# Contracting k and v over 128 rows instead of 64, with a new order of loads and new scheduler settings, in a fused linear attention and wave MLP kernel

## The chip, the cores and the metric

One Trainium2 chip, one of its cores. The metric is the device time of one execution in microseconds (us). A profile of one execution was taken for every kernel; its span (first to last instruction of the program) is some 1.8 us shorter than the device time. The tables give medians of all runs of a kernel. The experiments came with the kernel before in the same rounds, so kernels are compared by their ratios to it. PE is the matmul engine (PEld its weight loads), DVE the vector engine, ACT the scalar engine, POOL the GpSimd engine, SP the engine that issues the DMAs.

## The reference, cut to what matters

```python
# q, k, v: (8 batches, 8 heads, 576 tokens, 64), fp32
kv  = einsum('bhsd,bhse->bhde', k, v)      # 64x64 per head, contracts the 576 tokens
out = einsum('bhsd,bhde->bhse', q, kv)
x   = out / rms(out) * g_norm              # then (8, 576, 512)
theta = x @ w_theta
y = w_tok_r @ (x*cos(theta)) + w_tok_i @ (x*sin(theta))    # mixes the 576 tokens
u = x + y
result = u + relu(u @ w_ch)
```

The change touches the first line: 64 products of 576 tokens, in fp32, for 8 batches of 8 heads.

## The kernel before

The kernel is one static program. A scheduler in Python (`Weave`) takes tasks with a due time, engines, an assumed cost and what they need and use. It plays them through on a clock of its own, and so fixes the order of every engine's queue before anything runs. Where the scheduler believes PE idle in the first 40 us, it puts in a warm-up matmul (a `warm` task of 0.22 us that no one needs). The granted clock of the first 43.29 us is 1.00 with them in the trace of this kernel.

```python
PERIOD = 24.61
DUE = {"load": (-15.33, 2.93), ..., "attention": (1.6, 3.82), "norm": (12.64, 4.8), ...}   # cut
SLOTS = {..., "k": 6, "v": 6, "q": 6, ..., "wst": 8, ...}
class Weave:
    SLACK  = {"PE": 0, "ACT": 0.052, "DVE": 0.064, ...}
    MARGIN = {"PE": 0.011, "ACT": 0.06, "DVE": 0.119, ...}
```

k and v of a head pair are loaded with 64 partitions a head, 9 consecutive tokens a partition. Each head's product then runs in one 64x64 quadrant of PE; the two heads use the two quadrants of the diagonal.

```python
t = sb(kind, [P, NS, D], FP32, ...)            # NS = 9; partitions 0-63 head 0, 64-127 head 1
nc.sync.dma_start(out=t[:]..., in_=src[b, pair].rearrange("h (p j) d -> (h p) (j d)", j=NS))
...
for j in range(NS):                            # kv: 18 matmuls a head pair
    for r in range(2):
        half = slice(r * PH, (r + 1) * PH)
        nc.tensor.matmul(kvp[r*D:(r+1)*D, hp, :], st["k", b, hp][half, j, :],
                         st["v", b, hp][half, j, :], start=(j == 0), stop=(j == NS - 1))
weave.add(("kv", b, hp), [pe(0.6)], ...)       # assumed cost 0.6 us
```

x is turned (transposed on PE) in five pieces a batch; the fifth has 64 valid tokens and was turned with all 128 rows. The weights come in this order: batch 0, `w_theta`, the two mixers `w_tok`, batch 1, `w_ch`, batch 2.

## Time and profile before

| kernel before | |
|---|---|
| time, median of 4 runs | 242.91 us (242.85 to 243.21) |
| span of the profiled run | 241.2 us |
| first y matmul, last y matmul starts | 43.29 us, 232.94 us |
| kv groups (a head pair's kv), 32 of them | 36 PE instructions, 1.20 us each |

The first part of the profile page (busy us, share of the span, instructions) and its part 4 (the chain of work that ended last):

```profile
PE 233.1 (97%) x2789; PEld 160.3 (66%) x2789; DVE 183.3 (76%) x369; ACT 158.8 (66%) x297; POOL 86.3 (36%) x104
...
PE 92%; ACT 3%; DVE 3%; issue 0%; DVEq 0%
PE y L855 29%; PE kv L499 15%; PE vps L899 12%; PE th L768 11%; PE warm L284 9%; PE raw L535 4%; PE ups L890 4%; PE xTps L737 4%; PE th L773 2%; PE wTps L407 1%; ACT tr L811 1%; ACT tr L803 1%; PE qTps L469 0%; DVE f L784 0%; DVE ot L910 0%
```

PE is busy nearly always and is 92% of the chain. kv is 15% of it. The busy time in two stretches (columns: stretch, its length, then the busy us of PE, PEld, DVE, ACT and POOL with their instructions, granted clock, DMA share, GB/s):

```profile
68.40:79.00 10.60, 8.25 (x110) 5.81 (x109) 8.16 (x17) 7.39 (x16) 3.43 (x4) 1.00 0.95 323
79.00:198.00 119.00, 119.00 (x1529) 84.67 (x1527) 101.67 (x199) 88.09 (x161) 48.41 (x47) 1.00 0.66 190
```

In the long second stretch PE has no gap, and DVE, third in the row, is busy for 85% of the time. In the short first one PE loses 2.4 us. In the timeline of PE (start, duration, line, what, how many) a kv group and a turn of x look like this:

```profile
104.84 1.26 PE L499 MATMUL kv<-v,k 64*64 64x64 f32 x36
106.04 0.30 PE L890 MATMUL ups<-ident,uT 128*64 128x128 f16 x4
...
119.10 0.39 PE L737 MATMUL xTps<-ident,x 128*128 128x128 f16 x4
119.32 1.39 PE L855 MATMUL y<-wT,z 128*128 128x320 f16 x9
```

What an item takes from PE is the distance from its start to the start of the next, as durations overlap: 106.04 - 104.84 = 1.20 us for kv, 0.22 us for the turn. An fp32 matmul shows as two instructions, hence 36 for 18.

### The profile page before, as it was taken

To read this page: it belongs to the slowest core of one execution; us is meant where nothing else is said; L and a number is where in the kernel's file an instruction comes from. 1 tells how busy PE (TensorE), PEld (TensorE's weight loads), DVE (VectorE), ACT (ScalarE), POOL (GpSimd) and SP (SyncE) were. 2 spreads that over 40 slices of the span, in tenths; PEclk is the share of its full clock that TensorE was granted. 3 is DMA by queue.
4 is the path that set the end of the run, shared out by engine and by line. 5 is a ranking of instruction groups with operands and counts; after the bars stand their busy time and mean duration, and the time that the engine had idled before them with its cause. 6 is when DMAs were issued, how large, how long until landed. Compare 5 with 4: busy or idle time off the path is not lost.

```text
span 241.2 us, 6820 instructions
## 1 busy us (share of the span) xinstructions
PE 233.1 (97%) x2789; PEld 160.3 (66%) x2789; DVE 183.3 (76%) x369; ACT 158.8 (66%) x297; POOL 86.3 (36%) x104
## 2 busy tenths in 40 slices
PE   7999999999987999999999999999999999999993
PEld 2665556977655766776668766776676775765861
DVE  1267585288977889779897988997789868997652
ACT  2377677335885678647895868785858668788021
POOL 4005630354334560263363334433252605540000
PEclk9999999999999999999999999999999999999999
DMA  6995999974379748844796469974981512102314
GB/s 185 279 348 194 287 330 380 315 284 117 79 228 356 239 98 279 241 150 89 202 338 201 87 184 300 292 146 134 312 267 27 133 55 105 50 1 90 109 46 153
DMA packets 45375, 46.49 MB, mean 193 GB/s; under 512 B 21664, under 2 KB 30880, under 8 KB 45344
## 3 DMA queue, kind: packets, MB, share of 16 engines
q1 hardware_dynamic: 45280, 46.05, 62.7%
q8 instruction: 22, 0.36, 0.7%
q14 instruction: 9, 0.07, 0.1%
q0 software_dynamic: 64, 0.00, 0.0%
HBM read 33.06 MB, written 9.44 MB: 176 GB/s over the span
## 4 chain that ended last, share of the span: by engine, by line
PE 92%; ACT 3%; DVE 3%; issue 0%; DVEq 0%
PE y L855 29%; PE kv L499 15%; PE vps L899 12%; PE th L768 11%; PE warm L284 9%; PE raw L535 4%; PE ups L890 4%; PE xTps L737 4%; PE th L773 2%; PE wTps L407 1%; ACT tr L811 1%; ACT tr L803 1%; PE qTps L469 0%; DVE f L784 0%; DVE ot L910 0%; ACT sq L542 0%
## 5 line engine op out<-in xcount | busy, mean ns | idle before, releaser
L855 PE MATMUL y<-wT,z 128*128 128x320 f16 (+1 forms) x576 | 78.9, 286 | 1.5 <-DVE z L821 1.5
L855 PEld LDWEIGHTS <-z 128*128 128x128 f16 x576 | 53.7, 98 | 16.8 <-DVE z L821 2.0
L557 POOL TENSOR_TENSOR rt<-ss,mhalf 128x8 f32<-128x8 f32 x35 | 60.6, 1733 | 2.9
L863 DVE SCALAR_TENSOR_TENSOR uT<-y,gcol,xT 128x256 f16<-128x256 f32 (+1 forms) x64 | 32.7, 513 | 16.5 <-PE y L855 16.3
L553 POOL TENSOR_SCALAR ss<-ss 128x8 f32<-128x8 f32 x35 | 11.3, 323 | 94.4 <-DVE ss L546 93.8
L499 PEld LDWEIGHTS kv<-v,k 64*64 64x64 f32 x1152 | 36.1, 135 | 8.3 <-issue 6.1
L499 PE MATMUL kv<-v,k 64*64 64x64 f32 x1152 | 40.5, 221 | 0.0
L899 PE MATMUL vps<-wch,uT 128*128 128x512 f16 (+1 forms) x192 | 37.7, 344 | 0.0
L780 ACT ACTIVATE pt<-th,magic_t 128x512 f32<-128x512 f32 (+1 forms) x40 | 25.8, 644 | 18.0 <-PE th L768 17.2
L746 ACT ACTIVATE xT<-xTps,gcol 128x512 f16<-128x512 f16 (+1 forms) x36 | 22.9, 636 | 16.0 <-PE xTps L737 16.0
L768 PE MATMUL th<-wth,xT 128*128 128x512 f16 x128 | 32.8, 380 | 0.0
L784 DVE SCALAR_TENSOR_TENSOR f<-pt,th 128x512 f32<-128x512 f32 (+1 forms) x40 | 25.2, 629 | 9.0 <-ACT pt L780 8.9
L906 ACT COPY u<-ups 128x512 f16<-128x512 f16 (+1 forms) x40 | 21.3, 539 | 14.8 <-PE ups L890 14.5
L821 DVE TENSOR_TENSOR z<-x,tr 128x1024 f16<-128x1024 f16 (+1 forms) x40 | 25.2, 632 | 4.6 <-ACT tr L803 2.4
L910 DVE SCALAR_TENSOR_TENSOR ot<-vps,u 128x512 f32<-128x512 f32 (+1 forms) x40 | 25.1, 631 | 4.7 <-PE vps L899 2.2
L546 DVE TENSOR_REDUCE ss<-sq 128x8 f32<-128x512 f32 x36 | 24.3, 679 | 2.3 <-ACT sq L542 2.0
L569 DVE TENSOR_TENSOR x<-raw,rt 128x512 f16<-128x512 f32 x36 | 24.6, 683 | 1.3 <-POOL rt L557 1.1
L284 PE MATMUL warm<-kvbd 128*128 128x512 f16 x80 | 23.5, 411 | 1.7 <-DVE pio_t L248 1.5
L542 ACT ACTIVATE sq<-raw 128x512 f32<-128x512 f32 x36 | 21.1, 593 | 3.8 <-PE raw L535 3.8
L803 ACT ACTIVATE tr<-fa,pio_t 128x512 f16<-128x512 f32 x32 | 22.9, 719 | 0.8 <-DVE fa L791 0.2
L803 ACT ACTIVATE tr<-f 128x512 f16<-128x512 f32 x32 | 20.2, 632 | 2.9 <-DVE f L784 2.8
L899 PEld LDWEIGHTS <-uT 128*128 128x128 f16 (+1 forms) x192 | 14.2, 102 | 8.6 <-issue 0.6
(73 smaller groups left out, 217.0 us busy)
## 6 DMA issues: line engine op xcount, KB each, us to landing
k<-in_k_dram SPq DMA_DIRECT2D x32, 288.0 KB, 5.8
v<-in_v_dram SPq DMA_DIRECT2D x32, 288.0 KB, 5.8
q<-in_q_dram SPq DMA_DIRECT2D x32, 256.0 KB, 5.7
out_dram<-ot SPq DMA_DIRECT2D x32, 256.0 KB, 3.2
wmix<-in_moe_w_tok_r_dram SPq DMA_DIRECT2D x4, 288.0 KB, 6.7
wmix<-in_moe_w_tok_i_dram SPq DMA_DIRECT2D x4, 288.0 KB, 4.0
ql<-in_q_dram SPq DMA_DIRECT2D x8, 128.0 KB, 5.6
wst<-in_moe_w_theta_dram SPq DMA_DIRECT2D x4, 256.0 KB, 7.7
```

The costliest lines, as they stand in the source:

```text
L284: nc.tensor.matmul(t[:], kv_bd[1][:, 0, :], kv_bd[1][:].rearrange("p h c -> p (h c)"), start=True, stop=True,)
L499: nc.tensor.matmul(kvp[r * D:(r + 1) * D, hp, :], st["k", b, hp][half, j, :], st["v", b, hp][half, j, :], start=(j == 0), stop=(j == NS - 1),)
L557: nc.gpsimd.tensor_tensor(out=r[:], in0=t[:], in1=mhalf[:], op=ALU.pow)
L768: nc.tensor.matmul(t[:], xT[:, kc, :], wth[:, kc, :], start=(kc == 0), stop=(kc == NK - 1),)
L780: nc.scalar.activation(out=t[:], in_=st[th][:], func=AFT.Identity, bias=magic_t[:])
L784: nc.vector.scalar_tensor_tensor(out=t[:], in0=st[pt][:], scalar=MAGIC, in1=st[th][:], op0=ALU.subtract, op1=ALU.subtract,)
L803: nc.scalar.activation(out=t[:, which, :], in_=src[:], func=AFT.Sin, scale=-RAD, bias=0.0 if bias is None else bias[:],)
L821: nc.vector.tensor_tensor(out=t[:], in0=xb.unsqueeze(1).broadcast_to((P, w, C)), in1=st[tr][:, 0:w, :], op=ALU.mult,)
L855: nc.tensor.matmul(t[:], z[:, kc * P:(kc + 1) * P], wT[m][:, cols], start=(m == 0), stop=(m == NM - 1),)
L863: nc.vector.scalar_tensor_tensor(out=st["uT", b][:, kc, cols], in0=st[y][:], scalar=gcol[:], in1=st["xT", b][:, kc, cols], op0=ALU.mult, o ...
L899: nc.tensor.matmul(t[half], uT(kc), wch[:, kc, r * n:(r + 1) * n], start=(kc == 0), stop=(kc == NK - 1),)
L910: nc.vector.scalar_tensor_tensor(out=t[:], in0=st[vp][:], scalar=0.0, in1=st[u][:], op0=ALU.max, op1=ALU.add,)
```

## The change

Intent: PE is the limit, and a kv matmul in a quadrant uses only 64 of the 128 rows that could contract (64\*64 in its trace, where the matmuls of y show as 128\*128). Batches 1 to 7 load k and v over all 128 partitions with 4 tokens each (512 tokens), and the last 64 tokens as separate tails over 64 partitions; the other 64 partitions of the tail tiles stay zero. A pair then needs 10 matmuls for 18. Batch 0 keeps quadrants, as it would otherwise wait for a tail. Half of batch 1 is loaded ahead of the mixers, the tail of x is turned with 64 rows, and due times, slacks and costs of the scheduler are new.

```diff
-PERIOD = 24.61
+PERIOD = 24.57
     ... (15 of the 17 entries of DUE are new, e.g.)
-    "mixers": (20.83, 4.62),
-    "phase": (19.07, 4.95),
+    "mixers": (14.15, 5.87),
+    "phase": (19.49, 4.62),
-    "wst": 8,
+    "wst": 6,
+MIX_AFTER = 5        # mixers are loaded after head pair 1 of batch 1
+WCH_AFTER = 7
-    SLACK = {"PE": 0, "ACT": 0.052, "DVE": 0.064, ...}
-    MARGIN = {"PE": 0.011, "ACT": 0.06, "DVE": 0.119, ...}
+    SLACK = {"PE": 0.053, "ACT": 0, "DVE": 0.124, ...}
+    MARGIN = {"PE": 0.051, "ACT": 0, "DVE": 0.444, ...}
     ...
-                if kind == "q":
+                if kind == "q" or b > 0:         # [P, 2, NF, D]: 128 rows of NF = 4 tokens
     ...  (tails kl, vl: 128 KB each per batch, double-buffered)
+            if b > 0:
+                for j in range(NT):              # NT = 5: four of 512 tokens' rows, one tail
+                    for r in range(2):
+                        nc.tensor.matmul(
+                            kvp[r * D:(r + 1) * D, hp, :],
+                            st["k", b, hp][:, r, j, :] if j < NF else st["kl", b][:, 2 * hp + r, :],
+                            st["v", b, hp][:, r, j, :] if j < NF else st["vl", b][:, 2 * hp + r, :],
+                            start=(j == 0), stop=(j == NT - 1))
+                return
-        weave.add(("kv", b, hp), [pe(0.6)], ...
+        weave.add(("kv", b, hp), [pe(0.8 if b else 1.2)], ...
     ...  (turn of x)
+            rows = P if ti < NF else T
-                    t[:, kc, :], st[f"x{b}_{ti}"][:, kc * P:(kc + 1) * P], ident16[:],
+                    t[:, kc, :], st[f"x{b}_{ti}"][0:rows, kc * P:(kc + 1) * P], ident16[0:rows, 0:rows],
```

## The prediction

The 33 ns a matmul that it takes for the shorter turn of x is an estimate, the rate of kv's 64-column matmuls (1.20 us over 36 instructions).

> **What bounds the kernel now.** TensorE. The page has PE busy 233.1 of 241.2 us (97%), DVE 76%, ACT 66%; the chain that ended last is 92% PE, at full clock: y 29%, kv 15%, vps 12%, th 11%, and 9% warm-up matmuls in the load-bound start. By windows, from 79 to 198 us PE is never idle, DVE is busy 101.7 of 119 us (85%), DMA share 0.66. Exceptions: the start (first y at 43.3 us), a hole from 68 to 79 us (PE loses 2.4 us, chain on ACT and DVE), the drain after 198 us (4 us lost).
>
> **What changes.** In the timeline each kv group (one head pair) is 36 PE instructions, two fp32 passes of 18 matmuls in 64x64 quadrants, and takes 1.20 us, 33 ns each. In batches 1 to 7 (28 of 32 groups) 128 rows contract: 10 matmuls, 20 instructions, in 128x64 column tiles.
> - At 33 ns a group takes 0.67 us. [...] This trace's 128x64 tiles do run together, with a surcharge: the x8 tail th takes 0.56 us, 140 ns a pair, against 107 ns at full th's rate (215 ns per 512 columns). I take 0.75 us, between 0.67 and the 0.8 of the diff's cost table (its 1.2 for quadrants agrees with the trace). Saving 0.45 us per group.
> - About 24 groups run after the first y, in the busy stretch: -10.8 us. Those of batch 1 among warm-ups save nothing.
> - Tail x turn, 64 moving columns for 128: 56 to perhaps 33 ns a matmul, x4 x7: -0.6 us.
> - Half of batch 1 ahead of the mixers: DMA had a gap there (20 to 25 us: share 0.49), which the loads fill; mixers land later, but PE gets batch 1's kv meanwhile. The order after has 81 warm-ups against 80. First y: 42 to 45.5 us; cost +1.
> - DMA: k, v go from 2304 B runs to 1024 B, plus 14 tails of 128 KB in 256 B runs (the q tail takes 5.6 us to land, as long as 256 KB of q). Steady share about 0.75; not binding.
> - DVE and ACT lose nothing. With the steady stretch 7% shorter DVE goes from 85% to about 92%: new PE gaps, +1.5 us. Better costs in the scheduler may close part of the 68 us hole: -0.5.
>
> Sum: -9.4 us, so 233.5 us, range 229.5 to 238.5. Chances: faster by over 2% (below 238.0) 0.88, within 2% 0.11, slower 0.01.
>
> **What would show it.**
> - kv groups of batches 1 to 7 as x20, 0.67 to 0.8 us each, batch 0 still 1.20; kv's share of the chain near 10%.
> - Steady period (kv group to the same group a batch later, 24.8 us now) 23.0 to 23.5 us.
> - DVE busy sum near 183 us, over 90% in the steady stretch; PE slightly below 97%, with small idle ending on DVE or ACT.
> - First y within 2 us of 43.3.
>
> **What would make it wrong.** [...] (2) DVE's in-order queue becoming the limit: period near 24 us. (3) Mixers so late that the first y slips 4 us. (4) 256 B tails delaying loads in the DMA-bound stretch from 25 to 50 us. (5) Fast side: 0.67 us groups and smaller holes, near 229 us.

## The result, and the profile after

| | before | changed |
|---|---|---|
| time, median of 4 runs | 242.91 us (242.85 to 243.21) | 232.13 us (230.75 to 233.36) |
| span of the profiled run | 241.2 | 230.3 |
| first y starts | 43.29 | 44.32 |
| last y starts | 232.94 | 221.88 |
| PE time of kv after the first y | 29.9 | 17.6 |
| PE idle after the first y | 2.5 | 3.0 |
| warm-ups | 80 | 81 |

The ratio is 0.9552 (95% interval 0.9498 to 0.9607). Ratios here are the mean time of one kernel's fast runs over that of the other's in the same rounds, so not quite the ratio of the quoted medians. The rows on PE are worked out from the starts in the trace: what an instruction takes is the distance to the next start, up to 0.30 us, and what exceeds that is called idle.

The first part and part 4 of the page of the changed kernel:

```profile
PE 220.8 (96%) x2342; PEld 145.8 (63%) x2342; DVE 185.2 (80%) x368; ACT 157.3 (68%) x298; POOL 88.0 (38%) x108
...
PE 73%; DMA 9%; DVE 6%; ACT 5%; POOL 3%; issue 1%; SPq 1%; DVEq 0%
```

Its stretches, in the same columns as before:

```profile
68.00:79.00 11.00, 8.29 (x106) 6.23 (x104) 8.49 (x19) 6.46 (x14) 4.60 (x6) 1.00 0.92 275
79.00:187.00 108.00, 107.57 (x1185) 72.40 (x1182) 98.88 (x195) 84.42 (x158) 46.41 (x45) 1.00 0.78 205
```

PE still has almost no gap in the long stretch, but DVE is now at 98.88 of 108 us, 92%. The chain is only 73% PE, for two reasons. In the first 25 us it now goes through the loads (21 us of DMA, the 9% above), where it went through warm-ups before, though PE itself lost next to nothing by waiting for k and v (under 1 us in the whole run). In the long stretch it is 78% PE, 11% DVE, 5% ACT and 4% POOL, where it was all PE before. The hole near 70 us is still there, 2.7 us large. The timeline of PE of the changed kernel, with its first y, two kv groups in a row, the tail turn of x, and a single kv group:

```profile
44.32 2.14 PE L893 MATMUL y<-wT,z 128*128 128x256 f16 x18
...
62.02 0.69 PE L524 MATMUL kv<-v,k 128*64 128x64 f32 x16
62.53 0.29 PE L524 MATMUL kv<-vl,kl 128*64 128x64 f32 x4
62.65 0.64 PE L524 MATMUL kv<-v,k 128*64 128x64 f32 x16
63.12 0.29 PE L524 MATMUL kv<-vl,kl 128*64 128x64 f32 x4
63.34 1.04 PE L806 MATMUL th<-wth,xT 128*128 128x512 f16 x4
...
87.93 0.29 PE L775 MATMUL xTps<-ident,x 64*128 64x64 f16 x4
88.15 1.04 PE L937 MATMUL vps<-wch,uT 128*128 128x512 f16 x4
...
93.84 0.69 PE L524 MATMUL kv<-v,k 128*64 128x64 f32 x16
94.36 0.29 PE L524 MATMUL kv<-vl,kl 128*64 128x64 f32 x4
94.58 1.04 PE L937 MATMUL vps<-wch,uT 128*128 128x512 f16 x4
```

A kv group is now 20 instructions. It takes 0.74 us when it stands alone (93.84 to 94.58), but two in a row take only 1.32 us (62.02 to 63.34), with the first at 0.63. The tail turn takes 0.22 us (87.93 to 88.15), exactly as long as a turn of 128 rows before, and where a th matmul runs ahead of it, that one takes 311 ns for 216.

Where the 11.0 us of span come from is a short sum. The first y comes 1.0 us later; kv after the first y takes 12.4 us less of PE (29.93 to 17.56); PE idles 0.5 us more; all other matmuls after the first y take 0.2 us less in sum, and what follows the last matmul 0.1 us more. One of the groups behind the 12.4 us moved ahead of the first y (25 groups ran after it before, 24 now).

The distances from start to start inside one group, worked out from the trace in ns (the last number is the distance to the next, full-width instruction), show what a group consists of:

```
64x64 quadrants, 36:   7, 100,  7, 52,  6, 52,  7, 51, ... 7, 52, 6 | 151
128x64 columns,  20:   7, 100,  6, 52,  7, 51,  7, 51, ... 7, 51, 7 | 154
```

Two instructions of a pair start 7 ns apart, and pairs follow every 58 ns in both forms. So a pair costs the same whether 64 or 128 rows contract. Added to that are about 0.15 us inside the group, at its first pair (107 for 58) and its last (161 for 58). Where a full-width turn runs ahead of it, that turn's last matmul takes 149 ns for 56 as well. Together it is about 0.24 us a group. Next to another half-width group these additions vanish: an exit takes 51 instead of 154 ns. So in these traces the additions come with a change of the tile shape. It is not the fp32 type: fp16 matmuls in 128x64 tiles between full-width ones pay the same at their ends (149 ns ahead of them, 152 after), and from the last of such fp16 matmuls to a kv group behind them it is 52 ns. 0.24 us is what one such change and the way back cost here.

### The profile page after: what moved, and what is told of

Read it like the earlier page. It is cut to its first block, busy times and chain, and to the rows that moved or that the text cites. A ratio compares the mean times of both kernels' runs of the same rounds, so it can differ in the third digit from the quotient of the medians.

```text
span 230.3 us, 5955 instructions
## 1 busy us (share of the span) xinstructions
PE 220.8 (96%) x2342; PEld 145.8 (63%) x2342; DVE 185.2 (80%) x368; ACT 157.3 (68%) x298; POOL 88.0 (38%) x108
## 3 DMA queue, kind: packets, MB, share of 16 engines
q1 hardware_dynamic: 59840, 46.05, 71.9%
## 4 chain that ended last, share of the span: by engine, by line
PE 73%; DMA 9%; DVE 6%; ACT 5%; POOL 3%; issue 1%; SPq 1%; DVEq 0%
PE y L893 27%; PE vps L937 11%; PE th L806 11%; PE kv L524 6%; DMA wst<-in_moe_w_theta_dram 4%; PE xTps L775 4%; PE ups L928 4%; PE warm L293 3%; DMA vl<-in_v_dram 3%; PE raw L572 3%; DMA v<-in_v_dram 2%; POOL rt L594 2%; ACT tr L849 2%; DVE x L606 2%; PE wTps L432 2%; PE th L811 1%
## 5 line engine op out<-in xcount | busy, mean ns | idle before, releaser
L590 POOL TENSOR_SCALAR ss<-ss 128x8 f32<-128x8 f32 x35 | 9.5, 271 | 85.2 <-DVE ss L583 84.6
L859 DVE TENSOR_TENSOR z<-x,tr 128x1024 f16<-128x1024 f16 (+1 forms) x40 | 27.0, 674 | 3.4 <-ACT tr L849 1.7
L524 PE MATMUL kv<-v,k 128*64 128x64 f32 x448 | 19.0, 227 | 0.0
L524 PEld LDWEIGHTS kv<-v,k 128*64 128x64 f32 x448 | 15.3, 137 | 5.6 <-issue 4.2
```

The costliest lines, as they stand in the source:

```text
L524: nc.tensor.matmul(kvp[r * D:(r + 1) * D, hp, :], st["k", b, hp][:, r, j, :] if j < NF else st["kl", b][:, 2 * hp + r, :], st["v", b, hp][ ...
L859: nc.vector.tensor_tensor(out=t[:], in0=xb.unsqueeze(1).broadcast_to((P, w, C)), in1=st[tr][:, 0:w, :], op=ALU.mult,)
```

## The experiments

There were twelve runs, one of them the changed kernel again. The kernel before, in the rounds of each call, had medians from 243.14 to 243.39 us. The theory to be tested: the row form is the gain, by shortening kv on a PE-bound chain. The rivals: the new scheduler settings, or the new order of loads.

### 1. The row form alone, all but the row form, and two small parts

The kernel before with only the row form and its tails (`a_kv_only`):

```diff
 # kernel before, plus: loads of k, v for b > 0 in 128 rows; tails; the 10-matmul loop
 weave.add(("kv", b, hp), [pe(0.6)], ...)      # cost, due times, slacks, order of loads as before
```

> The kernel before with the 128-row form of k, v in batches 1 to 7 and the two tails added, and nothing else: its order of loads, its due times, slacks and costs (0.6 us a kv group) stay. Theory (the row form is the gain; 24 groups of batches 1 to 7 after the first y, each 0.47 us shorter on PE, nearly all of it on the chain): 231 to 234 us, 9 to 12 us below the kernel before. Rival (the retuned schedule and the order of loads make half of the gain or more): 237 us or above.

The changed kernel with quadrants (`b_quadrants`):

```diff
-                if kind == "q" or b > 0:
+                if kind == "q":
-            if b > 0:
+            if False:
-[pe(0.8 if b else 1.2)]
+[pe(1.2)]                                      # and no tails
```

> The changed kernel with quadrants for k, v of all batches (288 KB loads, no tails, 36 PE instructions and a cost of 1.2 us a group), everything else as changed. Theory: the gain is gone, 241 to 245 us. Rival (retune and order of loads): it stays near the changed kernel, 233 to 238 us.

The changed kernel with the mixers ahead of batch 1 (`c_mix_first`), and with the tail of x turned by 128 rows (`d_full_turn`):

```diff
-MIX_AFTER = 5
+MIX_AFTER = 3
```

> The changed kernel with the mixers loaded before all of batch 1, as in the kernel before (one constant, 5 becomes 3). Theory (the order of loads only moves waits about in the start; the first y moved from 43.3 to 44.3 us with the change): within 1.5 us of the changed kernel, first y between 42 and 45 us. Rival (the loads ahead are needed because kv of batch 1 would come too late): 2 us or more slower, first y or the second batch's first y later by that.

```diff
-            rows = P if ti < NF else T
+            rows = P                            # and its cost 0.25 for 0.13
```

> The changed kernel with the tail x turned by 128 rows as in the kernel before (eight times 4 transposes at 56 ns a piece, 0.22 us). In the changed kernel's trace the 4 shorter ones take 39, 29, 29 and then 122 ns to the next matmul, 0.22 us as well, with perhaps 0.1 us lost in the matmul ahead of them. Theory now (a change of tile shape costs what the shorter stream saves): within 1 us of the changed kernel, rather faster than slower, tail x turn again 0.22 us. Rival (my prediction: 0.6 us saved by 64 rows): 0.6 us slower than the changed kernel.

| run | median us | ratio to before | first y | last y |
|---|---|---|---|---|
| row form alone | 238.55 | 0.9809 (0.9783 to 0.9834) | 42.49 | 229.14 |
| all but the row form | 242.16 | 0.9958 (0.9935 to 0.9981) | 44.05 | 231.74 |
| mixers first | 233.42 | 0.9607 (0.9568 to 0.9646) | 39.72 | 223.55 |
| tail x by 128 rows | 232.67 | 0.9570 (0.9545 to 0.9596) | 43.53 | 222.29 |

The row form alone missed what was expected of it: 4.6 us faster, not 9 to 12. Everything except the row form is worth 1.0 us. So neither the theory nor the rival holds alone; 4.6 + 1.0 is about half of the gain. In the row-form run PE spends 11.1 us less on kv after the first y (18.8 for 29.9) but idles 7.9 us there for 2.5. Its waits (who waited for whom: total us, times, longest) say on what:

```profile
PEld L889 <- DVE z L855: 6.7, 4, 2.3
...
PE y L889 <- DVE z L855: 5.6, 4, 2.0
```

The same wait of the kernel before, from its own list:

```profile
PE y L855 <- DVE z L821: 1.5, 1, 1.5
```

y of a batch needs the last z of that batch, and z comes late in DVE's queue, whose order is fixed. Of the 11.1 us, 5.4 came back as idle time of PE, most of it waits for z (5.6 us for 1.5). Another 2.7 came back as other matmuls that took longer; this profile has a dip of the clock to half from 74.2 us, 3.4 us long (see the last part of this section). What is left, and a first y 0.8 us earlier, is the 3.8 us by which the last y is earlier.

The order of loads, as far as the place of the mixers goes, is worth about 1.3 us by the ratios (0.9607 - 0.9554 times 243, with the changed kernel of experiment 2), and the two intervals overlap. With the mixers first, y even starts 4.6 us earlier, contrary to the 42 to 45 us expected, but the stretch from first to last y is 6.3 us longer. Turning the tail of x with fewer rows is worth nothing that can be seen: 0.957 and 0.955 overlap. Its 0.6 us in the prediction were not there, as the four shorter matmuls (39, 29, 29 ns apart) are followed by 122 ns to the next, 0.22 us in all, and the matmul ahead loses 0.09 us more.

### 2. Which setting, and fewer changes of the tile shape

> The changed kernel itself, unchanged, so that the others of this call have it on the same chip, and for its spread (230.75 to 233.36 us in four runs, where the kernel before stays within 0.4 us). Both theories: 231 to 233.5 us, ratio near 0.955.

```diff
 # changed kernel with PERIOD and DUE of the kernel before        (r_due)
```

> The changed kernel with the table of due times and the period of the kernel before; slacks, costs, order of loads and the row form stay as changed. The row form alone gave only 4.6 us of the 10.8, although its trace has kv 13.2 us shorter on PE: PE idled 5.6 us more, mostly before y, waiting for z on DVE. Theory A (the order of the work, set by the due times, lets the freed PE time reach the end): 235 to 239 us, most of 5 us lost. Theory B (the slacks and margins of the scheduler do it): within 1.5 us of the changed kernel.

```diff
 # changed kernel with SLACK and MARGIN of the kernel before      (r_slack)
```

> The changed kernel with the slacks and margins of the kernel before; all else as changed. Theory A (due times): within 1.5 us of the changed kernel. Theory B (slacks and margins): 235 to 239 us. If both this and the run with the old due times lose 2 us or more, the settings only work together and neither is the cause by itself.

```diff
+KVG = 2                                         # (kv_pairs)
+                for h in range(hp - KVG + 1, hp + 1):    # two head pairs in one task
                     for j in range(NT): ...
-[pe(0.8 if b else 1.2)]
+[pe(1.4 if b else 1.2)]
```

> The changed kernel with kv of two head pairs in one go (40 PE instructions, cost 1.4 us), due when the second pair was. In the changed kernel's trace a pair of instructions takes 58 ns in both forms, and entering and leaving the half-width form from full 128x128 costs about 0.24 us a group beyond that (the matmul ahead 149 instead of 56 ns, the first pair 107 instead of 58, the last to the next 154 instead of 52). If that is a cost of changing the tile shape, each double group takes 1.32 us from its first start, 14 changes fewer save 14 x 0.24 = 3.4 us of PE and, as two thirds to all of freed PE time reach the end only with matching due times, 0.5 to 3 us of the whole. Rival (the gaps belong to each group's first load, whatever ran before): double groups of 1.46 us or more, no gain.

| run | median us | ratio to before |
|---|---|---|
| changed kernel again | 232.66 (231.68 to 232.99) | 0.9554 (0.9530 to 0.9577) |
| old due times | 234.80 | 0.9649 (0.9620 to 0.9677) |
| old slacks and margins | 233.69 | 0.9606 (0.9587 to 0.9624) |
| kv of two head pairs in one go | 234.91 | 0.9648 (0.9622 to 0.9674) |

By the medians, old due times lose 2.1 us, old slacks 1.0. Neither reaches the 235 to 239 us that theory A or B asked for, though the old due times come close. With the old due times PE waits for x, 4.8 us before the turn of x for 0.7 in the changed kernel (this profile is of the slowest of the six runs). First the line of the run with old due times, then that of the changed kernel:

```profile
PE xTps L775 <- DVE x L606: 4.8, 5, 2.8
...
PE xTps L775 <- DVE x L606: 0.7, 2, 0.5
```

The double groups did what the changes of shape predict, and lost all the same. One of them in the timeline of that run, 82.61 to 83.93 = 1.32 us:

```profile
82.61 0.69 PE L526 MATMUL kv<-v,k 128*64 128x64 f32 x16
83.12 0.29 PE L526 MATMUL kv<-vl,kl 128*64 128x64 f32 x4
83.24 0.64 PE L526 MATMUL kv<-v,k 128*64 128x64 f32 x16
83.71 0.29 PE L526 MATMUL kv<-vl,kl 128*64 128x64 f32 x4
83.93 0.82 PE L811 MATMUL th<-wth,xT 128*128 128x512 f16 x3
```

Over the whole run, PE's time on kv fell from 25.6 to 23.1 us, and PE's idle rose from 5.3 to 8.9. That makes 1.1 us of the 2.2 lost; the order also has 4 more warm-ups (85), and this profile has the clock at half for 6.8 us from 71.4 us. The waits of the run name x, which comes later because the first pair's kv is held back for the second:

```profile
PE xTps L780 <- DVE x L611: 4.8, 2, 4.5
```

### 3. The costs, and whether PE still bounds

kv summed over two of five row blocks only, a wrong result (`fewer`):

```diff
-                for j in range(NT):
+                for j in (0, NT - 1):
```

> Wrong on purpose: the changed kernel with kv of batches 1 to 7 summed over two of the five row blocks only (8 PE instructions a group for 20; loads, costs and therefore the whole order unchanged). A group falls from 0.73 to about 0.38 us, so PE has 24 x 0.35 = 8.4 us less after the first y. Theory A (PE still bounds, and in a fixed order freed PE time reaches the end in part only, as 4.6 of about 11.5 us did in the run with the row form alone): 2 to 5 us faster than the changed kernel. Theory B (DVE, with its in-order queue, is the limit by now): under 1 us faster. Theory C (all of it reaches the end): 7 us or more.

The changed kernel with the cost of kv as before (`r_cost`):

```diff
-[pe(0.8 if b else 1.2)]
+[pe(0.6)]
```

> The changed kernel with the cost of a kv group in the scheduler as before, 0.6 us for both forms (the traces have 0.73 and 1.20), all else as changed. It places 95 warm-ups for 81, as it thinks PE idle in the load-bound start when it is not. If costs are a part of what makes the row form pay, 1 to 3 us slower than the changed kernel; if only due times and slacks are, within 0.7 us.

| run | median us | ratio to before | first y | last y | warm-ups |
|---|---|---|---|---|---|
| two of five row blocks | 230.41 | 0.9458 (0.9437 to 0.9479) | - | - | 81 |
| kv costed 0.6 us | 237.35 | 0.9747 (0.9733 to 0.9760) | 47.20 | 227.48 | 95 |

(The profile of the first fell in a run with the clock at half from 36.1 and from 73.7 us, so no starts are given; the ratio is of fast runs.) A group takes 0.38 us for 0.73, so PE has 8.4 us less to do in the same order; that brings 2.3 us, from the ratios (0.9554 - 0.9458 times 243; the two intervals together leave some 0.8 us either way). Theory A: PE counts, but about a quarter of what it saves arrives.

The one false entry in the cost table loses 4.7 us, more than due times and slacks together. Of the 5.6 us by which its last y is later, 2.9 are there at the first y already: the scheduler believed PE idle and put 14 more warm-ups of 0.22 us into PE's queue in the start. PE spends 22.6 us on them before the first y, for 19.4. That they are what delays the first y is read from this match; no run took out warm-ups alone.

### 4. True costs added to the row form, and the double groups with a fitted order

```diff
 # row form alone, and                           (a_kv_cost)
-[pe(0.6)]
+[pe(0.8 if b else 1.2)]
```

> The run with the row form alone (238.55 us), with one thing more: the cost of a kv group in the scheduler, 0.8 us for 128 rows and 1.2 for quadrants, for 0.6; due times, slacks and order of loads stay as in the kernel before. Putting the false cost back into the changed kernel lost 4.7 us, 2.9 of them before the first y (14 more warm-ups). Theory A (true costs are most of what the row form alone lacks): 233.5 to 236 us. Theory B (true costs help only with the due times and slacks that were fitted to them): 237 us or above.

```diff
 # double groups, PERIOD, DUE, SLACK, MARGIN from a random search
 # in the scheduler's own account                            (kv_pairs_tuned)
```

> The run with kv of two head pairs in one go (234.91 us: PE spent 2.5 us less on kv, but PE waited 3.5 us more, for x), with due times, slacks and margins fitted to it anew by a random search in the scheduler's own account, which makes it 0.9 us shorter there than the changed kernel. Theory A (saved PE time reaches the end once the order fits): 230.5 to 232 us, at or below the changed kernel, PE idle between 5 and 7 us. Theory B (the other engines' waits are the limit by now, whatever PE saves): 232.5 us or above.

| run | median us | ratio to before | first y | last y | warm-ups |
|---|---|---|---|---|---|
| row form alone (from 1) | 238.55 | 0.9809 (0.9783 to 0.9834) | 42.49 | 229.14 | 83 |
| row form and true costs | 234.99 | 0.9668 (0.9636 to 0.9700) | 40.00 | 225.31 | 70 |
| double groups, fitted | 232.41 | 0.9551 (0.9532 to 0.9570) | 44.32 | 221.81 | 83 |

True costs are worth 3.4 us by the ratios (0.9809 - 0.9668 times 243). Theory A holds. Of the 3.8 us between the last y, 2.5 stand at the first y, with 13 warm-ups fewer. (True costs in the kernel before, with its quadrants and its own settings, were not run; all but the row form has them with the new settings, and gained 1.0 us.) The ladder is then: row form 4.6 us, with true costs 8.1, with due times, slacks and the order of loads 10.8, all from the ratios. The last step of 2.7 us is not split further; each part's removal from the whole (2.1 and 1.0 us for due times and slacks, about 1.3 for the loads) is of that size, but such removals need not add up.

The fitted double groups are the same as the changed kernel within noise. PE spends 1.8 us less on kv after the first y (15.8 for 17.6) and idles 1.5 us more. So no version here beats the changed kernel. I had stated 232.5 us or above for the rival, and 230.5 to 232 for the theory; 232.41 lies between. Together with experiment 3 it speaks for the rival: with DVE at 92% in the long stretch, saved PE time mostly becomes PE waits. That DVE's queue order is what sets the limit now is argued from these waits, not shown; no run here made DVE's work shorter, and PE itself is still busy 107.57 of 108 us in that stretch of the changed kernel.

### The spread of the changed kernel

The changed kernel spreads over 2.6 us in its first four runs, the kernel before over 0.4 (later, on another chip, the changed kernel over 1.3 us in 4 runs and the kernel before over 1.4 us in 11). The two profiles of the changed kernel agree to 0.07 us in the starts of kv and y from 24 to 71.9 us, and then part. Three stretches of the first profile (span 230.3):

```profile
68.00:71.50 3.50, 1.65 (x18) 1.04 (x16) 2.12 (x6) 3.40 (x9) 0.00 (x0) 1.00 0.77 178
71.50:75.00 3.50, 3.09 (x39) 2.35 (x39) 3.36 (x8) 0.84 (x2) 2.15 (x3) 1.00 0.96 310
75.00:78.50 3.50, 3.06 (x35) 2.38 (x37) 2.51 (x6) 1.73 (x3) 1.94 (x3) 1.00 1.00 323
```

and of the second (span 231.2):

```profile
68.00:71.50 3.50, 1.68 (x18) 1.07 (x16) 2.12 (x6) 3.40 (x9) 0.00 (x0) 1.00 0.88 203
71.50:75.00 3.50, 3.07 (x31) 2.34 (x32) 3.36 (x8) 0.87 (x2) 2.13 (x3) 0.65 1.03 335
75.00:78.50 3.50, 3.50 (x30) 2.69 (x29) 1.99 (x4) 1.17 (x2) 1.68 (x2) 0.86 1.06 346
```

The third number from the end, just ahead of the DMA share, is the granted clock: 0.65 and 0.86 for 1.00. In the clock record it is one dip to 0.5 from 72.6 us, 3.4 us long, right after the hole in which PE works 1.7 of 3.5 us. The last y is 0.93 us later in this run (222.81 for 221.88), which is all of the 0.93 us between the spans. In those later runs the clock goes with the time (0.996 granted at 231.68 us, 0.989 at 232.99). The spread of the first four runs it does not explain: all four list a granted clock of 1.0, with spans from 229.0 to 231.6 us, and what spreads them stays open. Dips of 3.4 us at 71 to 74 us are also in the profiles of the row form alone, with true costs, with old due times and with the full tail turn, and one of 6.8 us in the double groups; there is none in that of the kernel before. What sets a dip off is not shown: the two profiles of the changed kernel have the same hole ahead of it (PE busy 1.65 and 1.68 of 3.5 us), and one has the dip, the other not. The longest distance between two starts of PE ahead of the dip is 1.55 us.

## Why the prediction was right or wrong

It said 233.5 us (229.5 to 238.5) and the result is 232.13. The size of the sum held; one of its reasons held only under a condition that it did not name. In that it was lucky: the diff brought true costs and a new order along, which the sum counted as 0.5 us at most. The row form alone, on which the sum rests, runs at 238.55 us, 5 us above the stated sum and at the edge of the stated range. Smaller errors also went both ways (kv -12.4 us for -10.8, the turn 0 for -0.6, PE idle +0.5 for +1.5). The steady period held: a kv group of batches 3 to 7 comes 23.2 us after the same group a batch earlier on average (24.9 before; single distances in the changed kernel run from 19 to 30), within the stated 23.0 to 23.5.

- **kv group 0.75 us.** Measured 0.63 to 0.74, total kv after the first y 29.9 to 17.6 us. Right, and for a reason found later: a pair takes 58 ns in either form, plus about 0.24 us a group for changing the tile shape.
- **"About 24 groups run after the first y, in the busy stretch: -10.8 us."** The number fits the whole change (24 groups, PE's kv -12.4 us with the group that moved ahead). As a statement about the row form it was wrong: alone it brings 4.6 us; idle time, mostly waits for z, took back 5.4 of 11.1 us, and slower matmuls, some in a clock dip, 2.7. The prediction gave better costs "-0.5"; with the row form in place they are worth 3.4 us, and due times, slacks and loads another 2.7.
- **Tail x turn, -0.6 us.** Wrong, no gain: the term counted the shorter stream alone, and the change of shape takes it back, 0.22 us both ways.
- **First y 42 to 45.5 us, cost +1.** Measured 44.32, +1.03.
- **DVE to about 92%, PE gaps +1.5 us.** DVE 98.88 of 108 us, 92%, as said; PE idle rose by only 0.5 us after the first y.
- **The 68 us hole closes by 0.5.** Wrong, it went from 2.4 to 2.7 us, and in the second profile the dip behind it costs another 0.9.
- **DMA share about 0.75.** 0.78, from 0.66; not binding for kv: PE waited under 1 us for k and v in the whole run (1.2 us in the second profile).
- **kv near 10% of the chain.** 6%; the chain itself changed from 92% to 73% PE, about half of it through the loads in the start.

## What to carry to other kernels

Time freed on the busiest engine was only an offer here: the row form alone freed 11.1 us of PE's kv time after the first y and made the run 4.6 us faster. Whether it arrives depends on the order of the in-order queues around it, so re-fit the order, and first give the scheduler true costs, before judging a change by itself. A cost that is wrong by half for one task (0.6 for 1.20 us) hid 3.4 to 4.7 us here, much of it as filler work placed where there was no idle time. And the small half-width matmuls of kv cost PE less when they stand together (1.32 us for two groups in a row, 0.74 for one alone), as entering and leaving the shape once costs 0.24 us, as much as four pairs of 58 ns. No run here turned that saving into time: double groups lost 2.2 us with the old order and gained nothing with a fitted one.

## What else the traces show

- In the changed kernel column tiles on all 128 rows run at the same 58 ns a pair as the diagonal quadrants of the kernel before, and a weight load can overlap with a running matmul there (a load from 93.95 to 94.09 us under a matmul from 93.95 to 94.17, whose end is modelled). Each fp32 matmul with 64 columns shows as two instructions, and a pair of tiles as two steps of 58 ns.
- In the changed kernel the mixers' casts on POOL now fall among batch 0's z on DVE, of which four take 0.98 to 1.30 us (at most 0.69 in the kernel before), and several casts take 0.78 to 1.05 for 0.62. But z that run wholly under one of POOL's rt operations (1.67 us, reading ss in SBUF) still take 0.68 to 0.69 us, as at 58.78 us. What sets these pairs apart was not tested; the times of POOL in a trace are rough. In its timeline:

```profile
34.39 0.78 POOL L374 TENSOR_SCALAR wnat<-wmix 128x512 f16<-128x512 f32 x1
34.63 1.30 DVE L859 TENSOR_TENSOR z<-x,tr 128x1024 f16<-128x1024 f16 x1
35.15 0.23 POOL L374 TENSOR_SCALAR wtt<-wmix 128x64 f16<-128x64 f32 x1
35.35 1.05 POOL L374 TENSOR_SCALAR wnat<-wmix 128x512 f16<-128x512 f32 x1
```
